# Relays, loads and the norm's product handed to other engines, in a talking-heads attention with an MLP

## The chip, the core and the metric

The kernel runs on one core of one Trainium2 chip. The time is the device time of one execution in microseconds. The profile that is read here is one execution as the hardware profiler recorded it; its engines are PE (TensorE matmul), PEld (TensorE weight load), DVE (VectorE), ACT (ScalarE), POOL (GpSimd) and SP (SyncE). A name like SPq or POOLq means the engine's instruction queue, where DMA issues and waits stand.

## What is computed

q, k and v have 4 batches, 12 heads, 448 positions and 64 columns. Before and after the softmax, the 12 heads are mixed by a 12 x 12 matrix; the result goes through an MLP of 768 to 2048 to 768 with a leaky ReLU whose slope is learned.

```python
scores = scale * np.matmul(q, k.transpose(0, 1, 3, 2))
scores = np.einsum('bhij,hg->bgij', scores, w_pre)
attn = np.exp(scores - np.max(scores, axis=-1, keepdims=True))
attn = attn / (np.sum(attn, axis=-1, keepdims=True) + 1e-09)
attn = np.einsum('bhij,hg->bgij', attn, w_post)
x = np.matmul(attn, v)            # then to (1792, 768)
h = x @ w_in
out = (np.maximum(h, 0.0) + alpha * np.minimum(h, 0.0)) @ w_out
```

## The kernel before, in words

The query rows of a batch are cut into chunks: seven of 60 rows and one of 30 (it starts at row 418 and overlaps the one before). 32 chunks follow one another. The kernel is written as a loop over steps n; the order of the instructions on every engine is the order in which the loop writes them, and the framework adds the semaphore waits.

**Scores.** `qk(ci, p)` (L178) makes a third of a chunk's raw scores by matmuls (L185) and copies them from PSUM to `s_t[ci]` ("st") on ACT (L189). st has two buffers, so the copy for chunk ci waits until all relays have read chunk ci-2. In st a partition holds one query row of one half of the heads.

**Relays.** Mixing heads is a matmul whose contraction runs over heads, so heads and a few query rows must lie on partitions. `relay(n, dmas)` (L193) does this with DMAs from SBUF to SBUF: for group n (10 query rows, 12 heads) two transfers u = 0, 1 of 60 rows of 1792 bytes each take rows of st into `sr_b` ("sr"), six buffers in turn. For the short chunk, whose second half lies 60 partitions on, each transfer is made as two of 30 rows (L206, otherwise L203). At step n `relays(2*(n+RA+1), ...)` issues the two groups that the mix three steps later will read (RA = 3). There are 180 groups, two per step. All transfers of the loop stand on SP; the first four groups are shared by SP and ACT.

**Mix, exp, norm, post.** `mix(n)` (L210) multiplies two groups by `wk` (L213) and takes the negated row maximum on DVE (nm, L215). `exp(n)` (L217) runs on ACT and also gives the row sums. `norm(n-1)` (L568) adds 1e-9 and takes the reciprocal on DVE (L571, L572) and multiplies it into the second mixing matrix (r, L575): on GpSimd as long as the MLP's first tile is in work (`cur == 0`, which holds for 87 of 90 steps), on DVE after it. `post(n-2)` (L227) multiplies exp by r (L235) and copies the result to `a_t` on ACT (L241, L246).

**pv.** At the steps in `pv_at`, 16 times, `pv(due, hx)` multiplies by v (L258), adds two halves on ACT and DVE (xe, L271, L272), and leaves a store to the DRAM tile x2 (L275) in a list, `later`; `flush()` issues it on SP in the next step, behind the relays.

**Loads.** `load_q` (three buffers), `load_k` (one buffer for each p) and `load_v` (one for each hx) are issued on GpSimd. k and q for later chunks go through the list `loads`, which is worked off in the step after the qk that frees the buffer; the next batch's v is issued right behind the `pv` that frees it.

**Weights.** The MLP's weights come as 64-bit floats. `convert()` reads raw pieces by GpSimd DMAs (cr, L292), turns them into 32-bit floats by instructions on DVE (L60, L64 to L67) and GpSimd (L61, L62), and stores them to a DRAM tile wsc (L301). `load_w` reads them back (wr, L343) and `split_w` splits them into a rounded part (ACT, L356) and a rest (GpSimd, L357), "ws".

**MLP.** `moe(t)` is a generator for one batch (tile t): first matmul L413, second L447, three products of parts for each. `moe_work(n, amount)` runs it on until the step's budget of estimated PE time is used: PACE = 2000 ns a step while the first tile is in work, then 5400. It begins at a step after `ready[0]` (26 here), when the x of the first batch has been stored and read back (xr, L463) and split on DVE (xs, L476, L477). As long as `lead` holds, a step has no MLP work and four pieces of convert. What of the MLP is left after step 94 is run to its end alone.

A step writes, in this order: mix(n), relays, flush, loads, norm(n-1), pv if due, post(n-2), exp(n), qk, MLP and convert work. On GpSimd a step's queue therefore holds: loads of k and q, r, loads of v, then the weights' wr, ws, ce, wsc and cr.

Of the kernel before, what the change touches and what calls it, by code (L numbers as in the profile page):

```python
# [19 lines left out]
B, H, S, D = 4, 12, 448, 64  # L20
DM, DFF = 768, 2048
NT = B * S
HI = 5
# [4 lines left out]
CW = 60  # L28
# [42 lines left out]
def talking_heads_prelu(ctx: ExitStack, tc: tile.TileContext, q, k, v, w_pre, w_post, mask, w_in, w_out, alpha, out):  # L71
# [81 lines left out]
        age[next(i for i in range(4) if pairs[i] is t)] = clock[0]  # L153
        clock[0] += 1

    def load_k(b, p, dma=nc.gpsimd):
        k_t[b, p] = kp.tile([128, 2, S], F32, tag=f"k{p}", name=f"k{b}_{p}")
        src = k[b].rearrange("d (c r p j) -> r p d c j", r=2, c=2, j=S)
        for r in range(2):
            (dma if dma else (nc.sync, nc.scalar)[r]).dma_start(out=k_t[b, p][64 * r:64 * r + 64], in_=src[r, p])  # L160

    def load_q(ci, dma=nc.gpsimd):
        b, c = chunks[ci]
        n = NP * CHUNKS[c][1]
        q_t[ci] = q_b[ci % 3]
        src = q[b, :, q_off[c]:q_off[c] + 2 * n].rearrange("d (c r x) -> r d c x", c=2, r=2)
        for r in range(2):
            (dma if dma else (nc.sync, nc.scalar)[r]).dma_start(
                out=q_t[ci][64 * r:64 * r + 64, SR0:SR0 + n].rearrange("d (c x) -> d c x", c=2), in_=src[r])

    def load_v(b, hx):
        t = v_t[b, hx] = vp.tile([128, NS, DM // 2], F32, tag=f"v{hx}", name=f"v{b}_{hx}")
        nf = S // 128
        cols = slice(hx * (DM // 2), (hx + 1) * (DM // 2))
        nc.gpsimd.dma_start(out=t[:, :nf, :], in_=v[b, :nf * 128, cols].rearrange("(s p) n -> p s n", p=128))
        nc.gpsimd.dma_start(out=t[:S - nf * 128, nf, :], in_=v[b, nf * 128:, cols])

    def qk(ci, p, copy=nc.scalar.copy):  # L178
        b, c = chunks[ci]
        pt = grab()  # L180
        cn = CHUNKS[c][1]
        for cc in range(2):
            for r in range(2):
                h = slice(64 * r, 64 * r + 64)
                nc.tensor.matmul(pt[64 * cc:64 * cc + 64, r, :S], q_t[ci][h, (3 * cc + p) * cn + SR0 * cc:(3 * cc + p) * cn + SR0 * cc + 64],  # L185
                                 k_t[b, p][h, cc, :], start=True, stop=True)
        if p == 0:
            s_t[ci] = sp.tile([128, 2, 3, S], F32, tag="s", name=f"st{ci}")
        copy(s_t[ci][:, :, p, :], pt[:, :, :S])  # L189
        free(pt)  # L190
        done_qk.add((ci, p))
# [3 lines left out]
    def relay(n, dmas):  # L195
        ci, g = groups[n]
        nh = half(ci)
        t = sr_t[n] = sr_b[n % NSR]
        for u in range(2):
            p, o = SR0 + 2 * g + u, SR0 + HP * u  # L200
            dma = dmas[u % len(dmas)]
            if nh * HI == CW:
                dma.dma_start(out=t[o:o + HP], in_=s_t[ci][p:p + nh * (GI - 1) + 1:nh])  # L203
            else:
                for c in range(2):
                    dma.dma_start(out=t[o + HP // 2 * c:o + HP // 2 * (c + 1)], in_=s_t[ci][p + CW * c:p + CW * c + nh * (HI - 1) + 1:nh])  # L206

    def mix(n):
        to = m_t[n] = grab()
# [291 lines left out]
    with tc.manual_schedule():  # L501
# [37 lines left out]
            in1=wb[:, 1, :].rearrange("p (o g) -> p o g", o=1).to_broadcast([128, HI, H]),  # L539
            op=ALU.mult,  # L540
        )
        load_q(1)
        nc.gpsimd.dma_start(out=alpha_sb, in_=alpha)
        conv = convert()
        relayed = 0
# [22 lines left out]
        def norm(n):  # L568
            se = se_t.pop(n)
            s1 = sm.tile([128, 2], F32, tag="s1", name=f"s1{n}")  # L570
            nc.vector.tensor_scalar_add(s1, se, 1e-9)  # L571
            nc.vector.reciprocal(out=s1, in_=s1)  # L572
            r = rp.tile([128, 2, HP], F32, tag="r", name=f"r{n}")
            wf = wq.rearrange("p (o g) i -> p o (g i)", o=1)
            (nc.gpsimd if cur == 0 else nc.vector).tensor_tensor(r, wf.to_broadcast([128, 2, HP]),  # L575
                                    s1.rearrange("p (u o) -> p u o", o=1).to_broadcast([128, 2, HP]), ALU.mult)
            r_t[n] = r

        def moe_work(n, amount):
            nonlocal cur, budget  # L580
            budget += amount
            while budget > 0 and cur < len(TB):
                if tasks[cur] is None:
                    if n <= ready[cur] + 1:
                        budget = 0.0
                        return
                    for _ in (nxt_x[cur] if cur in nxt_x else split_x(cur)):
                        pass
                    if cur == 1:
                        converts(conv_steps)  # L590
                        cvs.close()
                        wops.append(ctx.enter_context(tc.tile_pool(name="wop2", bufs=2, reuse_waits="tile")))
                    tasks[cur] = moe(cur)
# [5 lines left out]
        def step(n):  # L599
            step_now[0] = n  # L600
            if n in (0, 1):
                load_q(n + 2)
            if n in (2, 3):
                load_v(0, n - 2)
            due = pv_at.get(n)
            lead = n <= ready[0] + 1
            pace = 0.0 if lead else PACE[min(cur, 2)]
            if live(n):
                mix(n)
            if n >= 0:  # L610
                relays(2 * (n + RA + 1), (nc.sync,))
            flush()
            for f, *args in loads:
                f(*args)
# [3 lines left out]
            if due is not None:  # L618
                b = pvs[due][0]
                for hx in range(2):  # L620
                    pv(due, hx)
                    if due + 1 < len(pvs) and pvs[due + 1][0] != b:
                        load_v(b + 1, hx)
            if live(n - LAG):
                post(n - LAG)
            if live(n):
# [74 lines left out]
```

## Time and profile before

| what | us |
|---|---|
| runs, median (lowest to highest of 3) | 1000.92 (992.66 to 1004.43) |
| the profiled execution | 996.11 |
| its span from first to last instruction | 994.3 |

The mean granted TensorE clock of the profiled execution was 0.945 of full speed. In the rows below, times are microseconds from the span's start unless marked ns. A row of a wait reads: engine and what it was about to do, then after the arrow what ended the wait, the sum in us, how often, and the longest. The names before and after an arrow of an instruction are what it writes and what it reads.

### The profile page before, as it was taken

What the parts mean: (1) busy time and instruction counts of PE and PEld (TensorE: products, weight loads), DVE (VectorE), ACT (ScalarE), POOL (GpSimd) and SP (SyncE); (2) the same over time, 40 slices, a digit from 0 to 9 for tenths busy, and PEclk for the clock granted to TensorE, in tenths of its full rate; (3) what the DMA queues carried; (4) which work ended last, traced back from release to release, by engine and by line L of the source; (5) the groups of instructions that cost most, each with busy time, mean ns of one, the idle gap of its engine ahead of it and who ended that gap; (6) DMA issues with size and microseconds to landing.
All of it is one profiled execution on the core that took longest, in us unless ns stands there. A gap on an engine that the chain in (4) does not pass through costs nothing.

```text
span 994.3 us, 27470 instructions
## 1 busy us (share of the span) xinstructions
PE 859.1 (86%) x11532; PEld 666.7 (67%) x11532; DVE 598.4 (60%) x990; ACT 429.1 (43%) x780; POOL 561.8 (57%) x713
## 2 busy tenths in 40 slices
PE   6688666587889979787799988999999999999997
PEld 2354444254647657464566657899988999889996
DVE  4468545468657788873665444645476565764564
ACT  2357455435456556453465753523223233133231
POOL 6456535626667675765572411556664766567661
PEclk7789889869989999897999999999999999999999
DMA  6777757736687686676665534343346433444422
GB/s 176 193 217 221 185 159 249 217 117 192 183 213 232 191 264 190 202 194 174 190 196 162 161 118 164 93 124 112 107 115 186 127 112 110 125 152 119 111 80 72
DMA packets 74603, 161.71 MB, mean 163 GB/s; under 512 B 26277, under 2 KB 56113, under 8 KB 74481
## 3 DMA queue, kind: packets, MB, share of 16 engines
q0 software_dynamic: 25408, 103.16, 37.2%
q1 hardware_dynamic: 48216, 55.59, 17.9%
q8 instruction: 91, 1.49, 0.6%
q10 hardware_dynamic: 856, 1.21, 0.4%
q14 instruction: 32, 0.25, 0.1%
HBM read 97.62 MB, written 23.59 MB: 122 GB/s over the span
## 4 chain that ended last, share of the span: by engine, by line
PE 54%; DMA 15%; DVE 14%; POOL 8%; issue 5%; ACT 3%; SPq 0%; POOLq 0%; ACTq 0%; DVEq 0%
PE p L413 19%; PE p L447 17%; DMA sr<-st 8%; PE p L258 7%; PE p L235 4%; PE p L213 4%; PE p L185 4%; POOL ws L357 3%; DVE nm L215 2%; DMA xr<-x 2%; DVE acc L379 2%; DMA x<-xe 1%; DVE g L371 1%; DVE xs L477 1%; DVE t L364 1%
## 5 line engine op out<-in xcount | busy, mean ns | idle before, releaser
L357 POOL TENSOR_TENSOR ws<-wr,ws 128x768 fp32r<-128x768 f32 x128 | 236.7, 1850 | 179.0 <-ACT ws L356 178.1
L413 PE MATMUL p<-xs,ws 128*128 128x448 f32 x1152 | 254.0, 374 | 9.8 <-DVE xs L476 9.4
L447 PE MATMUL p<-g,ws 128*128 128x448 f32 x1152 | 247.4, 370 | 8.6 <-POOL ws L357 5.2
L413 PEld LDWEIGHTS p<-xs,ws 128*128 128x128 f32 x1152 | 216.3, 191 | 53.1 <-issue 27.0
L447 PEld LDWEIGHTS p<-g,ws 128*128 128x128 f32 x1152 | 215.7, 189 | 39.2 <-POOL ws L357 7.9
L356 ACT CAST ws<-wr 128x768 fp32r<-128x768 f32 x128 | 104.0, 838 | 196.0 <-issue 114.1
L235 PEld LDWEIGHTS p<-r,e 64*64 64x64 f32 x5040 | 104.0, 138 | 80.8 <-POOL r L575 50.4
L215 DVE TENSOR_REDUCE nm<-p 128x2 f32<-128x896 f32 x90 | 97.7, 1085 | 90.1 <-PE p L213 87.4
L185 PE MATMUL p<-k,q 64*64 64x448 f32 x768 | 113.5, 610 | 37.6 <-ACT st L189 14.8
L235 PE MATMUL p<-r,e 64*64 64x60 f32 x5040 | 110.1, 226 | 37.6 <-POOL r L575 27.8
L222 ACT ACTIVATE e<-p,nm 128x448 f32<-128x448 f32 x180 | 112.6, 635 | 59.0 <-DVE nm L215 38.8
L241 ACT COPY at<-p 128x960 f32<-128x960 f32 x88 | 86.7, 985 | 106.1 <-PE p L235 104.9
L213 PE MATMUL p<-sr,wk 64*64 64x448 f32 (+1 forms) x720 | 109.1, 597 | 24.4 <-DMA sr<-st 12.2
L364 DVE TENSOR_SCALAR t<-p,alpha_sb 128x448 f32<-128x448 f32 x64 | 43.4, 679 | 139.2 <-PE p L413 139.2
L379 DVE TENSOR_TENSOR acc<-p,acc 128x896 f32<-128x896 f32 x84 | 90.4, 1084 | 41.7 <-PE p L447 41.7
L189 ACT COPY st<-p 128x896 f32<-128x896 f32 x95 | 84.5, 912 | 70.4 <-DMA sr<-st 55.6
L575 POOL TENSOR_TENSOR r<-wq,s 128x120 f32<-128x120 f32 x87 | 38.4, 442 | 130.2 <-DVE s L572 108.3
L258 PEld LDWEIGHTS p<-at,v 64*64 64x64 f32 x2688 | 82.3, 141 | 20.9 <-ACT e L222 9.4
L343 POOL DMA_DIRECT2D wr<-wsc x128 | 72.0, 563 | 42.5 <-POOL ws L357 30.8
L258 PE MATMUL p<-at,v 64*64 64x120 f32 (+1 forms) x2688 | 84.9, 273 | 10.4 <-ACT e L222 5.5
L371 DVE TENSOR_TENSOR g<-t,g 128x448 fp32r<-128x448 f32 x64 | 74.2, 1200 | 2.1 <-ACT g L370 2.1
L213 PEld LDWEIGHTS p<-sr,wk 64*64 64x64 f32 (+1 forms) x720 | 28.2, 141 | 66.4 <-issue 23.4
(49 smaller groups left out, 676.8 us busy)
## 6 DMA issues: line engine op xcount, KB each, us to landing
wr<-wsc POOLq DMA_DIRECT2D x128, 384.0 KB, 3.5
sr<-st SPq DMA_DIRECT2D x332, 105.0 KB
cr<-in_w_in_dram POOLq DMA_DIRECT2D x32, 384.0 KB, 6.0
cr<-in_w_out_dram POOLq DMA_DIRECT2D x32, 384.0 KB, 5.2
wsc<-ct POOLq DMA_DIRECT2D x64, 192.0 KB, 4.2
xr<-x SPq DMA_DIRECT2D x24, 224.0 KB
out_dram<-acc SPq DMA_DIRECT2D x12, 448.0 KB
q<-in_q_dram POOLq DMA_DIRECT2D x54, 90.0 KB, 5.2
```

Of the source, the lines that this page charges most:

```text
L185: nc.tensor.matmul(pt[64 * cc:64 * cc + 64, r, :S], q_t[ci][h, (3 * cc + p) * cn + SR0 * cc:(3 * cc + p) * cn + SR0 * cc + 64], k_t[b, p][ ...
L213: nc.tensor.matmul(to[hf:hf + 64, u, :S], wk[r, :], g[r, :], start=True, stop=True)
L215: nc.vector.tensor_reduce(out=nm, in_=to[:, :, :S], axis=AX.X, op=ALU.max, negate=True)
L222: nc.scalar.activation(out=e_t[n][:, u], in_=m_t[n][:, u, :S], func=AF.Exp, bias=nm_t[n][:, u:u + 1], scale=1.0, accum_out=se_t[n][:, u:u ...
L235: nc.tensor.matmul(dst[:, :, HI * u:HI * u + HI], e[h, u, 64 * jb:64 * jb + 64], r[h, u].rearrange("p (h i) -> p h i", h=H), start=True, s ...
L241: nc.scalar.copy(at[:, :, col:col + 2 * GI].rearrange("p q (g i) -> p g q i", g=2), pt[:, :, :NS * GP].rearrange("p g (q i) -> p g q i", i ...
L258: nc.tensor.matmul(to[64 * t:64 * t + 64, r, cl * cn:(cl + 1) * cn], v_t[b, hx][pr, s, (2 * cl + t) * D:(2 * cl + t + 1) * D], a_t[pr, s, ...
L356: nc.scalar.copy(t[:, 0], w)
L357: nc.gpsimd.tensor_tensor(t[:, 1], w, t[:, 0], ALU.subtract)
L379: nc.vector.tensor_tensor(dst, pt[:, :, :N], dst, ALU.add)
L413: nc.tensor.matmul(pt[:, f % 2, :S], w[:, tw, c * 128:(c + 1) * 128], xs[:, tx, c, :], start=(j == 0), stop=(j == 3 * NCC - 1))
L447: nc.tensor.matmul(pt[:, d, :S], w[:, tw, (c + d) * 128:(c + d + 1) * 128], g[:, tg], start=(j == 0), stop=(j == 3 * FG - 1))
```

## The change

Five things are changed. (1) In the loop, relays are issued with the list (SP, GpSimd): transfer u = 0 of each group on SP, u = 1 on GpSimd. (2) q of a short chunk is loaded 30 columns further on, so that its rows in st lie in one regular pattern, and the short chunk's transfer is one of 60 rows, not two of 30. (3) q, k and v are issued on SP, all through the list `loads`, which a step works off behind its relays and its x stores; the load of chunk 1's q before the loop stays on GpSimd. (4) norm's product is always on DVE. (5) The MLP's first work and the end of `lead` come one step later.

```diff
-    def load_k(b, p, dma=nc.gpsimd):
+    def load_k(b, p, dma=nc.sync):
...
-    def load_q(ci, dma=nc.gpsimd):
+    def load_q(ci, dma=nc.sync):
...
-                out=q_t[ci][64 * r:64 * r + 64, SR0:SR0 + n].rearrange("d (c x) -> d c x", c=2), in_=src[r])
+                out=q_t[ci][64 * r:64 * r + 64, 64 - CHUNKS[c][1]:64 - CHUNKS[c][1] + n].rearrange("d (c x) -> d c x", c=2), in_=src[r])
...
-        nc.gpsimd.dma_start(out=t[:, :nf, :], in_=v[b, :nf * 128, cols].rearrange("(s p) n -> p s n", p=128))
-        nc.gpsimd.dma_start(out=t[:S - nf * 128, nf, :], in_=v[b, nf * 128:, cols])
+        nc.sync.dma_start(out=t[:, :nf, :], in_=v[b, :nf * 128, cols].rearrange("(s p) n -> p s n", p=128))
+        nc.sync.dma_start(out=t[:S - nf * 128, nf, :], in_=v[b, nf * 128:, cols])
...
         for u in range(2):
-            p, o = SR0 + 2 * g + u, SR0 + HP * u
-            dma = dmas[u % len(dmas)]
-            if nh * HI == CW:
-                dma.dma_start(out=t[o:o + HP], in_=s_t[ci][p:p + nh * (GI - 1) + 1:nh])
-            else:
-                for c in range(2):
-                    dma.dma_start(out=t[o + HP // 2 * c:o + HP // 2 * (c + 1)], in_=s_t[ci][p + CW * c:p + CW * c + nh * (HI - 1) + 1:nh])
+            p, o = 64 - CHUNKS[chunks[ci][1]][1] + 2 * g + u, SR0 + HP * u
+            dmas[u % len(dmas)].dma_start(out=t[o:o + HP], in_=s_t[ci][p:p + nh * (GI - 1) + 1:nh])
...
-        load_q(1)
+        load_q(1, nc.gpsimd)
...
-            (nc.gpsimd if cur == 0 else nc.vector).tensor_tensor(r, wf.to_broadcast([128, 2, HP]),
+            nc.vector.tensor_tensor(r, wf.to_broadcast([128, 2, HP]),
...
-                    if n <= ready[cur] + 1:
+                    if n <= ready[cur] + 2:
...
             if n in (0, 1):
-                load_q(n + 2)
+                loads.append((load_q, n + 2))
             if n in (2, 3):
-                load_v(0, n - 2)
+                loads.append((load_v, 0, n - 2))
...
-            lead = n <= ready[0] + 1
+            lead = n <= ready[0] + 2
...
-                relays(2 * (n + RA + 1), (nc.sync,))
+                relays(2 * (n + RA + 1), (nc.sync, nc.gpsimd))
...
-                        load_v(b + 1, hx)
+                        loads.append((load_v, b + 1, hx))
```

## Rows read from the trace of the kernel before

**Rows 1.** The page: busy time of each engine, and granted clock in 40 slices

```profile
PE 859.1 (86%) x11532; PEld 666.7 (67%) x11532; DVE 598.4 (60%) x990; ACT 429.1 (43%) x780; POOL 561.8 (57%) x713
...
PEclk7789889869989999897999999999999999999999
```

**Rows 2.** Busy time by stretch: length; PE, PEld, DVE, ACT, POOL; clock, DMA share, GB/s

```profile
30.00:180.00 150.00, 107.73 (x2496) 69.95 (x2496) 86.46 (x184) 82.38 (x164) 82.32 (x140) 0.86 0.70 203
180.00:215.00 35.00, 19.60 (x275) 12.53 (x273) 15.57 (x34) 9.09 (x19) 12.22 (x22) 0.66 0.67 198
215.00:600.00 385.00, 327.71 (x6086) 227.37 (x6081) 255.28 (x463) 211.14 (x406) 223.84 (x329) 0.96 0.65 188
...
650.00:994.00 344.00, 335.33 (x1777) 307.46 (x1769) 197.33 (x228) 94.90 (x134) 210.01 (x172) 1.00 0.41 118
```

**Rows 3.** The chain that ended last: shares by engine, then pieces (start, us, what)

```profile
PE 54%; DMA 15%; DVE 14%; POOL 8%; issue 5%; ACT 3%; SPq 0%; POOLq 0%; ACTq 0%; DVEq 0%
...
117.42 14.09 DMA sr<-st
...
444.07 14.54 DMA sr<-st
```

**Rows 4.** Who waited for whom, the whole span: us in total, times, longest

```profile
POOL r L575 <- DVE s L572: 108.3, 37, 16.4
...
ACT st L189 <- DMA sr<-st: 55.6, 10, 13.8
...
PE p L235 <- POOL r L575: 27.8, 17, 4.5
...
PE p L185 <- ACT st L189: 14.8, 4, 7.5
...
PE p L213 <- DMA sr<-st: 12.2, 4, 4.8
...
PE p L185 <- DMA k<-in_k_dram: 10.9, 6, 4.2
...
PE p L213 <- ACT st L189: 4.3, 3, 2.3
```

**Rows 5.** Groups of instructions, shapes apart: busy us, mean ns | idle before

```profile
L215 DVE TENSOR_REDUCE nm<-p 128x2 f32<-128x896 f32 x90 | 97.7, 1085 | 90.1 <-PE p L213 87.4 <-ACT ws L356 2.6
...
L575 POOL TENSOR_TENSOR r<-wq,s 128x120 f32<-128x120 f32 x87 | 38.4, 442 | 130.2 <-DVE s L572 108.3 <-PE p L185 14.7 <-PE p L258 5.8
...
L168 POOL DMA_DIRECT2D q<-in_q_dram x62 | 38.2, 626 | 15.9 <-PE p L185 8.1 <-DMA v<-in_v_dram 2.3 <-PE p L258 2.0
...
L175 POOL DMA_DIRECT2D v<-in_v_dram x8 | 6.2, 776 | 0.0
L176 POOL DMA_DIRECT2D v<-in_v_dram x8 | 4.4, 552 | 0.0
...
L575 DVE TENSOR_TENSOR r<-wq,s 128x120 f32<-128x120 f32 x3 | 0.8, 283 | 0.2
```

**Rows 6.** Tile sr, its instructions: ns min/median/max, first and last start

```profile
L213 PEld LDWEIGHTS p<-sr,wk x720: 129/133/228, 18.1 to 628.4; 64*64 64x64 f32 x169, 60*64 60x64 f32 x11
...
L203 SPq DMA_DIRECT2D sr<-st x332: 762/767/1647, 12.4 to 613.7; - x166
L206 SPq DMA_DIRECT2D sr<-st x48: 741/746/773, 122.1 to 479.1; - x48
```

**Rows 7.** DMA issues on the page: count, KB each, us from issue to landing

```profile
q<-in_q_dram POOLq DMA_DIRECT2D x54, 90.0 KB, 5.2
```

**Rows 8.** DMA queues from 108 to 132 us: packets, MB, share of 16 engines

```profile
q0 software_dynamic: 1008, 3.74, 59.4%
q1 hardware_dynamic: 1726, 1.78, 26.9%
...
k<-in_k_dram POOLq DMA_DIRECT2D x6, 224.0 KB, 9.5
...
q<-in_q_dram POOLq DMA_DIRECT2D x2, 90.0 KB, 9.3
```

More of the change, by code (lines that the diff above doesn't have):

```diff
@@ L184, in qk @@
                 h = slice(64 * r, 64 * r + 64)
-                nc.tensor.matmul(pt[64 * cc:64 * cc + 64, r, :S], q_t[ci][h, (3 * cc + p) * cn + SR0 * cc:(3 * cc + p) * cn + SR0 * cc + 64],
+                nc.tensor.matmul(pt[64 * cc:64 * cc + 64, r, :S], q_t[ci][h, (3 * cc + p) * cn + (64 - cn) * cc:(3 * cc + p) * cn + (64 - cn) * cc + 64],
                                  k_t[b, p][h, cc, :], start=True, stop=True)
```

## The prediction, made before the change was run

> **What bounds the kernel now.** I read the page first, then the busy time of each engine by stretch, the chain of waits, the list of who waited for whom, the groups of instructions, and last the DMA queues.
>
> The page shows PE busy for 859.1 of 994.3 us, and DVE and POOL near 60% [rows 1]. The mean hides two different stages. From 650 us on only the MLP is left: PE is busy for 335 of 344 us at full clock [rows 2], and nothing that the diff touches runs there. Before that the attention runs, with some MLP work put between its steps by a fixed budget. From 30 to 180 us PE is busy for 107.7 of 150 us, from 180 to 215 us for 19.6 of 35, from 215 to 600 us for 327.7 of 385: idle 42, 15 and 57 us. DMA is 65 to 70% busy in all three, and PE's granted clock is below full in the first two (0.86 and 0.66) [rows 1, 2]. So whatever the change gains lies in these 115 us of idle PE and in the lower clock beside them. PE's work itself is only moved in time: what isn't done between steps is done after them.
>
> The chain shows where the idle time comes from. DMA holds 15% of it, and its longest pieces are waits for relays of some 14 us, as at 117 and 444 us [rows 3]. The waits give the totals. ACT's copies into st (L189) waited 55.6 us for relays to have read the old st. PE idled 27.8 us for r from POOL (17 times), 14.8 and 4.3 us for those st copies, 12.2 us for sr directly and 10.9 us for k [rows 4]: 70 us that the change aims at by its place. All sums below are made against the profiled execution's own 996.11 us, which is 0.5% under the median of the runs, 1000.92.
>
> **Part 1: norm's product from POOL to DVE.** It removes 87 instructions from POOL, 38.4 us, and adds 87 to DVE at the 283 ns that three such instructions already take there: 24.6 us [rows 5]. The product's inputs come from DVE itself, so a hop between engines goes too, and r no longer stands behind POOL's subtractions (ws) and DMA issues. What reads r is post(n-2), one step later; on DVE r is ready a step before it. Of the 27.8 us of PE idle I count 20 as gained, since in the lead-in, where the chain runs through DVE itself, the next wait is close behind. Bounds: 0 to -28. The price is DVE time. DVE has 14% of the chain, 139 of its 598 busy us [rows 1, 3], so 23% of an added microsecond lies on the path: 24.6 x 0.23 = +6 us. Bounds: 0 (all hidden beside PE) to +24.6 (all of it on the path).
>
> **Part 2: half of the relays begun by POOL, short chunks in one transfer.** There are 384 relay transfers now: 332 and 48 on SP, 4 on ACT [rows 6]. The 48 halves become 24, so 360. The first six groups keep 12 on SP and ACT; of the other 348, SP and POOL begin 174 each. On SP a step's four relays take 4 x 0.767 = 3.07 us to issue one after the other, and for the short chunks eight halves take 8 x 0.746 = 5.97 us [rows 6]; with two on each of two engines it is 1.53 us on SP. What is released last, the st copy or the sr that mix reads, comes some 1.5 us earlier, and 4.4 us earlier in a short chunk's steps.
>
> On POOL the trace has no relay. Its DMA issues take 552 to 776 ns by the rows of v, and 626 for q [rows 5]; I take 0.60 us, near q's, the transfer nearest in size: 174 x 0.60 = 104 us (96 to 135). Taken off POOL: 38.4 us of products and the issues of 60 q, 18 k and 16 v, 94 x 0.626 = 58.8 us by q's row. Net +7 us of 562 busy (-1 to +38), so POOL is hardly fuller. It gets no longer wait either: now it waits 108.3 us in all, 37 times, for DVE's reciprocal before r [rows 4], which on DVE stands behind the reduction of the same step's mix. A relay on POOL waits for the mix alone, which is earlier. Behind it queue POOL's ws subtractions and wr loads, the same that queue behind r now.
>
> What lies on the path: 14.8 + 4.3 + 12.2 = 31.3 us of PE idle from relays. The long stalls are where transfers on POOL's queue crowd the relays' queue. From 108 to 132 us POOL's queue q0 holds the 16 DMA engines 59.4% of the time and SP's q1 26.9% [rows 8], and six k loads and two q loads were issued on q0 there. Afterwards k, q and v stand on q1, half of the relays on q0, and every step's relays ahead of that step's loads. I count half of the 31.3, -16 us; bounds 0 to -31 if the transfers only change places, and above zero as the second rival has it.
>
> The Trainium skill speaks against this part. "DMA: Bandwidth & Descriptors" (Rules for kernel authors) says that spreading DMAs over SP, ACT and GpSimd doesn't help bandwidth, as all run on the same 16 engines, and saves only issue time. The trace agrees that both queues share the engines (59.4% and 26.9% in one window); it doesn't show yet whether order alone removes a 14 us stall. By the rule the -16 would be only the issue time, and this is the first rival.
>
> **Part 3: q, k and v on SP behind the step's relays and stores.** 94 issues leave POOL and stand on SP: 94 x 0.77 = 72 us on an engine that keeps 182 of its 380 relay issues (174 and 8 ahead of the loop) and so loses 198, 152 us. POOL's own waits before such loads go too: 8.1 us before q, and 14.7 us that L575 waited for L185's matmuls, which k and q loads ahead of it wait for [rows 5]. On SP a load waits for matmuls of the previous step; the next step's relays, queued behind it, need the later mix anyway. k must still land before the next chunk's scores: of its 10.9 us I count -3 (bounds +10.9, as much again if k waits behind relays and stores on one queue, to -10.9).
>
> **Part 4: one more step of lead.** The MLP starts one step later, so 2000 ns (PACE[0]) of PE work move behind the attention: +2 us and no more. Less if that work met a PE that idled anyway: the other bound is -15, all idle PE of 180 to 215 us, where the MLP starts [rows 2].
>
> **Clock.** The 107.7 us of PE work from 30 to 180 us ran at a granted 0.86, so for part of the time at 1.2 GHz and not 2.4; at full clock it would be some 15 us shorter, and the lower level stands in the stretches with most idle PE [rows 2]. I take -4 (0 to -15). **New lateness.** Relays on POOL's queue stand behind wr and cr loads there. A 90 KB q load on it landed 5.2 us after issue [rows 7], and POOL is at times a step late. I take +5, a quarter of the 19.1 us that PE idled for the st copies (0 to the second rival's size).
>
> Sum: -20 + 6 - 16 - 3 + 2 - 4 + 5 = -30 us, so 966 us against the profile, a ratio of 0.970. On the median of 1000.92 that is **970 us**, the prediction. The terms' own spread makes this case 955 to 985.
>
> **Rivals.**
> 1. *Bytes bound the relays.* For it: the DMA engines were 86% busy in the window above [rows 8], and no byte is taken away. Against: over the attention the share is 65 to 70% [rows 2], and the stalls are few and long. Then the relay and k terms vanish (+19), and so does the clock's (+4) and the new lateness (-5): -12 us, 989 on the median.
> 2. *POOL's relays come too late; slower.* Place: the st copy of each chunk, L189, mostly one step after the last relays of the chunk two before. A step is about 6.8 us (90 mixes from 18.1 to 628.4 us [rows 6]), and that copy comes into the next one, behind a reduction of 1.1 us [rows 5] and two exps (I put 3 us for it all), so it decides from where a POOL relay lands over 9 us after its mix. For it: r stands where these relays will stand in POOL's order, and PE met it late 17 times [rows 4]; 5.2 us of landing leaves little [rows 7]. Against: POOL waited for DVE at that point 37 times, so it was in time then. If each of 30 chunks waits 5 us there, ACT's wait goes from 55.6 to 150 us. PE idled 19.1 of those 55.6 us, a third, so PE's idle grows by 32: -20 + 6 + 2 + 32 = +20, 1021. "SBUF — State Buffer" (the engine ports) of the Trainium skill names a mechanism that would add to this: GpSimd can't write a DMA's descriptors while VectorE holds a port that they share. The rows so far don't show it in the issue times, 552 to 776 ns on average with DVE 60% busy [rows 1, 5].
> 3. *More than counted.* The 70 us of aimed waits go nearly whole, with the clock: -28 + 6 - 31 - 8 + 2 - 8 = -67 by the bounds; -55 taken as reachable, 946.
> 4. *Nothing.* The r wait is replaced by one for DVE's longer queue and relays stay as they are: -10 + 6 + 2, 999.
>
> **How the numbers follow.** Forecast 0.47, rival 1 0.18, rival 2 0.17, rival 3 0.12, rival 4 0.06. Over 1% either way (991 and 1011) is about what a measurement of this kernel can tell from no change, as its three runs lie 1.2% apart. The forecast and rival 3 are faster; of rival 1, which sits at the edge, 0.12, in all 0.71. Same: 0.06 of rival 1, 0.05 of rival 2 in a mild form and 0.05 of rival 4, in all 0.16. Slower: the rest of rival 2 and a little of rival 4, 0.13. The range leaves out half of rival 3 and two thirds of rival 2, together under 2 in 10: 945 to 1004.
>
> **What would show it.** Right: L575 on DVE 90 times at about 283 ns and PE's wait for r under 5 us; POOL with 174 relay issues near 0.6 us and about as busy as now; ACT's wait for relays at L189 under 30 us, with no piece of over 10 us in the chain; granted clock before 215 us higher; the MLP from its lone stage on unchanged in length. Wrong: a landing of POOL's relays over 9 us, L189 waiting over 55 us, or idle PE before DVE's max reduction (nm) grown by the added DVE work; unchanged long relay pieces with DMA share unchanged mean rival 1.

## The result and the profile after

The changed kernel takes 1010.84 us (median of 13 runs, 1003.47 to 1019.48), against 997.92 for the kernel before in the runs beside it. The ratio is 1.0132, 95% interval 1.0097 to 1.0168: slower by 1.3%, on the other side of no change than the forecast of 970 and outside its range. The profiled execution took 1003.47 us, its span 1001.7. It is the shortest of the 13, so the two profiles lie 7.4 us apart where the medians lie 12.9 apart.

A ratio on record takes only the runs within 1.5% of a kernel's shortest, and beside e5 to e12 one very short run of the kernel before (984.6 and 984.8 us) therefore makes the cut drop 16 of its 29 and 7 of its 17 runs, which puts these eight ratios 0.4 to 0.6% too high beside the others. So a second figure stands with a ratio where it matters: "by all runs" is the mean of all runs of a kernel over that of the kernel before beside it, which lies between 997.4 and 1000.0 us each time. For the changed kernel it is 1.0139; outside e5 to e12 the two figures differ by 0.12% at most.

The page of the kernel after (busy time; granted clock; shares of the chain that ended last; the issues of relays on POOL) answers to [rows 1, 3, 7].

```profile
PE 866.3 (86%) x11532; PEld 673.7 (67%) x11532; DVE 619.8 (62%) x1077; ACT 429.4 (43%) x780; POOL 565.0 (56%) x706
...
PEclk7689899689889999898988998999999999999999
...
PE 47%; DMA 15%; DVE 13%; issue 11%; POOL 9%; ACT 3%; SPq 1%; POOLq 0%; ACTq 0%; DVEq 0%
...
sr<-st POOLq DMA_DIRECT2D x174, 105.0 KB, 5.7
```

Span less busy time gives PE's idle time: 135.4 us after, 135.2 before. It has not shrunk, and the same 11532 matmuls kept PE busy 7.2 us longer, at a mean granted clock of 0.934 where it was 0.945. DMA still holds 15% of the chain.

By stretch (columns as in [rows 2]), the kernel after:

```profile
30.00:180.00 150.00, 113.95 (x2664) 72.49 (x2656) 96.50 (x224) 88.15 (x178) 87.53 (x147) 0.90 0.79 215
180.00:215.00 35.00, 18.02 (x333) 13.82 (x333) 18.44 (x44) 10.55 (x23) 10.36 (x18) 0.66 0.63 180
215.00:600.00 385.00, 329.64 (x5936) 229.21 (x5935) 266.50 (x502) 204.85 (x392) 221.15 (x320) 0.93 0.67 183
...
650.00:994.00 344.00, 340.36 (x1808) 311.85 (x1807) 202.91 (x233) 96.02 (x136) 215.29 (x177) 1.00 0.41 118
```

Ahead of 180 us the change works: 2664 matmuls instead of 2496 in the same 150 us, at a higher clock. From 215 to 600 us 150 fewer are done (5936 for 6086), at a lower clock, and what is missing is done at the end. So a gain and a loss lie in different stages. Not all of either is the relays' doing; the experiments part them.

Who waited for whom, the kernel after (us in total, times, longest), answering to [rows 4]:

```profile
POOL ws L352 <- ACT ws L351: 214.0, 77, 20.8
...
POOL sr L201 <- PE p L208: 44.9, 18, 7.0
...
ACT st L189 <- DMA sr<-st: 37.3, 8, 8.8
...
PE p L208 <- DMA sr<-st: 18.8, 8, 4.6
...
PE p L185 <- ACT st L189: 16.3, 4, 6.2
...
PE p L230 <- ACT st L189: 11.8, 3, 4.7
...
PE p L185 <- DMA k<-in_k_dram: 11.1, 6, 5.4
PE p L253 <- ACT st L189: 9.2, 3, 4.5
PE p L230 <- DVE r L570: 8.9, 8, 3.9
```

PE's wait for r fell from 27.8 to 8.9 us. In its place PE waits for the st copies: L230 (post) and L253 (pv) together 21.0 us, where before only pv had such a wait, one of 2.5 us; and L185 16.3. The relays themselves cost PE 18.8 us for 12.2. And POOL's longest wait is for ACT's casts, before its ws subtraction: 214.0 us. POOL waited for a mix before a relay only 18 times in 87 steps (44.9 us); mostly the mix had ended before POOL came to its relays. In the view that gave [rows 4], the wait for the casts was already POOL's largest, a row that the prediction did not read; the second row is pv's one wait:

```profile
POOL ws L357 <- ACT ws L356: 178.1, 74, 12.2
...
PE p L258 <- ACT st L189: 2.5, 1, 2.5
```

The st copies and r by form, and the relays of tile sr, kernel after, answering to [rows 5, 6]; the first row is the kernel before, whose row for the st copies [rows 5] leaves out:

```profile
L189 ACT COPY st<-p 128x896 f32<-128x896 f32 x95 | 84.5, 912 | 70.4 <-DMA sr<-st 55.6 <-PE p L185 4.5 <-DMA x<-xe 4.0
...
L189 ACT COPY st<-p 128x896 f32<-128x896 f32 x95 | 84.7, 913 | 91.2 <-DMA sr<-st 37.3 <-DMA k<-in_k_dram 18.6 <-PE p L185 12.7
...
L570 DVE TENSOR_TENSOR r<-wq,s 128x120 f32<-128x120 f32 x90 | 28.2, 313 | 3.1
```

```profile
L201 SPq DMA_DIRECT2D sr<-st x182: 762/790/1781, 13.9 to 616.5; - x182
L201 POOL DMA_DIRECT2D sr<-st x174: 547/586/782, 35.7 to 614.2; - x174
...
DMA to landing us min/median/max: 2.1/5.7/10.1
```

ACT's idle time before L189 grew from 70.4 us to 91.2, though the part that relays end by the profile fell from 55.6 to 37.3. POOL's issues cost what was forecast, 0.589 us each; their landing reaches 10.1 us (the trace has the landings of POOL's transfers, not of SP's).

What that looks like in one stretch of the timeline of the kernel after (start, length, engine; an issue "x2" is two transfers):

```profile
518.43 0.98 PE L208 MATMUL p<-sr,wk 64*64 64x448 f32 x8
...
519.42 1.62 SPq L201 DMA_DIRECT2D sr<-st  x2
...
519.58 1.82 POOL L352 TENSOR_TENSOR ws<-wr,ws 128x768 fp32r<-128x768 f32 x1 [10.20 <-ACT ws L351]
...
522.30 1.85 POOL L352 TENSOR_TENSOR ws<-wr,ws 128x768 fp32r<-128x768 f32 x1
...
523.04 0.98 PE L208 MATMUL p<-sr,wk 64*64 64x448 f32 x8
...
523.48 0.53 SPq L175 DMA_DIRECT2D v<-in_v_dram  x1
...
525.08 1.19 POOL L201 DMA_DIRECT2D sr<-st  x2
...
526.11 0.54 SPq L176 DMA_DIRECT2D v<-in_v_dram  x1
...
526.76 1.76 SPq L201 DMA_DIRECT2D sr<-st  x2
...
529.77 1.18 POOL L201 DMA_DIRECT2D sr<-st  x2
...
533.14 1.71 ACT L189 COPY st<-p 128x896 f32<-128x896 f32 x2 [5.95 <-DMA sr<-st]
...
534.10 1.86 PE L230 MATMUL p<-r,e 64*64 64x60 f32 x54 [4.17 <-ACT st L189]
```

The mix of a step ends at 519.41. SP begins its two relays 0.01 us later. POOL's two stand in its queue behind two ws subtractions, the first of which has waited 10.20 us for ACT's casts, and are begun at 525.08, 5.67 us later. The next mix ends at 524.02. Now SP is late too, since it is issuing loads of v until 526.65: its relays begin at 526.76, POOL's at 529.77. At 533.14 the st copy has waited 5.95 us for a relay to finish, and post's matmuls start at 534.10 after PE has idled 4.17 us for that copy.

Counted over steps 27 to 86 of the timeline, from the end of a step's mix to the end of its last relay's issue, median and 90th percentile: in the kernel after 1.7 and 4.1 us on SP, 5.3 and 11.9 us on POOL; with all four relays on SP (e6, below) 3.8 and 8.8. In steps 0 to 26, ahead of the MLP, the medians after are 2.2 on SP and 4.0 on POOL, and 6.6 in e6. So POOL is late in both stages. Ahead of the MLP four relays on SP alone are later still; after its start they are not.

What stands in front of POOL's relays can be counted too. Over steps 27 to 86 of the kernel after, the time from the end of a mix to the start of POOL's first relay is 291 us in all, 4.1 at the median. Of it 84 us go to the conversion's ce (29 of them waiting for DVE), 78 to ws (21 waiting for ACT's casts), 99 to issues of wr, wsc and cr, and 23 to relays of the step before. So the MLP's own ws and wr are 117 us of it, and the conversion (ce, wsc, cr), which stands in the queue ahead of the MLP too, is half.

### The profile page after: what moved, and what is told of

It reads as the page before. It is cut to its first block, busy times and chain, and to the rows that moved or that the text cites. A ratio compares the mean times of both kernels' runs of the same rounds, so it can differ in the third digit from the quotient of the medians.

```text
span 1001.7 us, 27286 instructions
## 1 busy us (share of the span) xinstructions
PE 866.3 (86%) x11532; PEld 673.7 (67%) x11532; DVE 619.8 (62%) x1077; ACT 429.4 (43%) x780; POOL 565.0 (56%) x706
## 4 chain that ended last, share of the span: by engine, by line
PE 47%; DMA 15%; DVE 13%; issue 11%; POOL 9%; ACT 3%; SPq 1%; POOLq 0%; ACTq 0%; DVEq 0%
PE p L408 17%; PE p L442 16%; DMA sr<-st 5%; PE p L253 4%; POOL ws L352 4%; PE p L230 3%; PE p L185 3%; DMA xr<-x 3%; PE p L208 3%; DMA cr<-in_w_out_dram 3%; DVE nm L210 2%; DMA k<-in_k_dram 2%; POOL sr L201 1%; DVE acc L374 1%; DMA wr<-wsc 1%
## 5 line engine op out<-in xcount | busy, mean ns | idle before, releaser
L352 POOL TENSOR_TENSOR ws<-wr,ws 128x768 fp32r<-128x768 f32 x128 | 236.3, 1846 | 215.0 <-ACT ws L351 214.0
L408 PE MATMUL p<-xs,ws 128*128 128x448 f32 x1152 | 251.3, 372 | 1.8 <-DVE xs L471 0.8
L230 PEld LDWEIGHTS p<-r,e 64*64 64x64 f32 x5040 | 107.8, 140 | 65.0 <-issue 28.6
L185 PE MATMUL p<-k,q 64*64 64x448 f32 x768 | 118.0, 631 | 37.7 <-ACT st L189 16.3
L201 POOL DMA_DIRECT2D sr<-st x174 | 100.6, 589 | 73.5 <-PE p L208 44.9
L230 PE MATMUL p<-r,e 64*64 64x60 f32 x5040 | 112.6, 228 | 25.8 <-ACT st L189 11.8
L208 PE MATMUL p<-sr,wk 64*64 64x448 f32 (+1 forms) x720 | 109.4, 593 | 24.8 <-DMA sr<-st 18.8
L189 ACT COPY st<-p 128x896 f32<-128x896 f32 x95 | 84.7, 913 | 91.2 <-DMA sr<-st 37.3
L253 PE MATMUL p<-at,v 64*64 64x120 f32 (+1 forms) x2688 | 88.7, 279 | 29.0 <-ACT e L217 16.0
L253 PEld LDWEIGHTS p<-at,v 64*64 64x64 f32 x2688 | 85.1, 145 | 39.5 <-ACT e L217 18.8
L61 POOL TENSOR_SCALAR ce<-ce 128x384 int32<-128x384 int32 x64 | 35.4, 554 | 80.7 <-DVE ce L60 78.0
```

The costliest lines, as they stand in the source:

```text
L201: dmas[u % len(dmas)].dma_start(out=t[o:o + HP], in_=s_t[ci][p:p + nh * (GI - 1) + 1:nh])
L208: nc.tensor.matmul(to[hf:hf + 64, u, :S], wk[r, :], g[r, :], start=True, stop=True)
L230: nc.tensor.matmul(dst[:, :, HI * u:HI * u + HI], e[h, u, 64 * jb:64 * jb + 64], r[h, u].rearrange("p (h i) -> p h i", h=H), start=True, s ...
L253: nc.tensor.matmul(to[64 * t:64 * t + 64, r, cl * cn:(cl + 1) * cn], v_t[b, hx][pr, s, (2 * cl + t) * D:(2 * cl + t + 1) * D], a_t[pr, s, ...
L352: nc.gpsimd.tensor_tensor(t[:, 1], w, t[:, 0], ALU.subtract)
L408: nc.tensor.matmul(pt[:, f % 2, :S], w[:, tw, c * 128:(c + 1) * 128], xs[:, tx, c, :], start=(j == 0), stop=(j == 3 * NCC - 1))
```

## The experiments

All ratios are to the kernel before on the same chip, with 95% intervals. A quotient of two of them carries about 0.005 to 0.006 either way.

**Each part alone, then all but one.** Edits are the parts of the diff above. For r on DVE alone (e1), and for the relays (e2) alone:

```
-            (nc.gpsimd if cur == 0 else nc.vector).tensor_tensor(r, ...
+            nc.vector.tensor_tensor(r, ...
...
-                relays(2 * (n + RA + 1), (nc.sync,))
+                relays(2 * (n + RA + 1), (nc.sync, nc.gpsimd))
```

> The kernel before, with only norm's product moved to DVE for all steps. Theory A (relays begun by GpSimd land too late; the product's move is a gain): 8 to 20 us faster than before, PE's wait for r below 10 us. Theory B (loads on SP hold up the relays behind them; the product's move is about neutral): within 5 us. Theory C (DVE's queue is what got longer): 5 to 10 us slower, ACT's wait for nm in exp grown from 39 us to over 50.

> The kernel before, with only the second transfer of each group begun by GpSimd in the loop (short chunks still in halves). Theory A: 15 to 30 us slower than before, GpSimd's relays landing in 5 us or more at the median and ACT's wait for relays at L189 at or above 56 us. Theory B: within 5 us of before, as the relays alone are not what was held up. Theory C: within 5 us.

> The kernel before, with only q, k and v loaded by SP behind each step's relays and stores. Theory A: within 5 us, or faster by up to 10 as GpSimd loses 94 issues and its waits for L185. Theory B: 10 to 20 us slower, with relays queued behind k and v in the chain. Theory C: within 5 us.

> The kernel before, with only the first MLP work and the end of lead one step later. Theories A and B: 0 to 3 us slower (2000 ns of PE work moved behind the attention). Theory C, in which the pacing is what costs: 5 to 10 us slower.

> The kernel before, with only the short chunk's q moved and its relays made in one transfer of 60 rows. Theory A2 (the single parts are harmless or helpful except the relays on GpSimd, and the loss of the whole change is their interplay): 0 to 6 us faster, as 24 issues of 0.75 us go. Theory D (the short chunk's new shape itself is slow, for it puts all of a transfer's rows on another pattern): 5 to 15 us slower.

Measured: r alone 0.9857 [0.9815, 0.990]; half of the relays on POOL alone 1.0088 [1.005, 1.0127]; q, k, v on SP alone 0.9978 [0.995, 1.0007]; one more step of lead alone 1.0023 [0.9987, 1.0058]; short chunks in one transfer alone 1.0053 [1.0011, 1.0095], which by all runs is 0.9996 (± 0.003), so a cost of these transfers is not shown. Added up they make no change on record (-1.4 + 0.9 - 0.2 + 0.2 + 0.5 = 0.0%) and -0.4% by all runs, and all together cost 1.3%.

r does what was forecast. The waits of e1:

```profile
PE p L185 <- DMA k<-in_k_dram: 9.5, 6, 4.5
...
PE p L235 <- DVE r L575: 5.7, 6, 1.7
```

and of e2, where r still stands on POOL:

```profile
PE p L235 <- POOL r L575: 63.6, 27, 5.8
...
ACT st L189 <- DMA sr<-st: 15.7, 3, 8.9
```

There the relays do shorten ACT's wait, 55.6 to 15.7 us, but r, behind relay issues on POOL, makes PE wait 63.6 us for 27.8. Theory A had e1 right and the direction of e2, but had expected 15 to 30 us lost there (9 measured) and ACT's wait at 56 us or more. Theory B's loss of 10 to 20 us from the loads alone is not there.

> The changed kernel with the loop's relays all on SP again. Theory A2: 10 to 20 us faster than the kernel before, close to norm's product alone (987). Theory E (r on DVE loses its gain as soon as loads stand on SP): within 5 us of the kernel before or slower.

> The changed kernel with q, k and v loaded by GpSimd again at their old places, relays still half on GpSimd. Theory A2: slower than the kernel before by 0 to 10 us, so the loss stands with the relays. Theory F (loads on SP and half of the relays on GpSimd are each harmless and collide only together): 10 to 15 us faster than the kernel before, since e2 lost its time in r on GpSimd, which is on DVE here.

> The changed kernel with norm's product on GpSimd again while the first tile is in work. Theory A2: 15 to 30 us slower than the kernel before, PE's wait for r over 50 us. Theory G (r on DVE is worth nothing once the relays stand on GpSimd): the same time as the changed kernel within 5 us.

Measured: the change without relays on POOL (all on SP) 0.9945 [0.990, 0.9991], by all runs 0.990; without the loads on SP 0.9981 [0.9934, 1.0028], by all runs 0.993; without r on DVE 1.0266 [1.0201, 1.033], by all runs 1.021. Beside the other parts, relays on POOL cost 1.9% on record (1.0132 / 0.9945) and 2.4% by all runs; the loads on SP cost 1.5% and 2.1%; r gains 1.3% and 0.7% (each by all runs ± 0.5 or 0.6). e6 lies between theories A2 and E on record and near A2 by all runs (10 us faster); e7 fits neither A2 nor F; e8 is as slow as A2 said, with a wait of PE for r of 48.9 us.

**Which property of the relays: k loads in their way, their number, or the engine?** Theory F1 held that the k loads now on SP delay relays, F2 that each relay on POOL costs. Edits to the changed kernel: k back on POOL (e9); the relays' second queue on ACT (e10); all relays on POOL (e11).

```
+    def load_k(b, p, dma=nc.gpsimd):
...
+                relays(2 * (n + RA + 1), (nc.sync, nc.scalar))
...
+                relays(2 * (n + RA + 1), (nc.gpsimd,))
```

> The changed kernel with k alone loaded by GpSimd again; q and v stay on SP. Theory F1 (the loss is that SP's relays stand behind bulk loads of k on SP's queue while GpSimd's queue, now with relays beside the weights, takes more of the DMA engines): half or more of the 1.3% comes back, within 5 us of the kernel before. Theory F2 (a relay begun by GpSimd lands late whatever SP carries, and that is all): no change against the changed kernel, 8 to 18 us slower than before.

> The changed kernel with the second transfer of each group begun by ACT instead of GpSimd. F1 and F2 both expect GpSimd's queue to be as free as in the run without relays on it; ACT pays 174 issues of 0.8 us, 139 us on an engine 43% busy. If two queues for relays are worth anything by themselves, 5 to 15 us faster than before; if ACT's issue time and its waits for the mix stand in the way of exp and the copies, 10 us slower or more.

> The changed kernel with both transfers of each group begun by GpSimd in the loop, SP left with loads and stores: the dose doubled. F2: about twice the loss that the GpSimd relays cost with loads on SP (1.9%), so 25 us slower than before or more, ACT's idle before L189 over 110 us. F1: no relay stands behind k any more, so no slower than the changed kernel, within 5 us of it.

Measured: e9 1.0172 [1.0119, 1.0224], e11 1.0165 [1.0115, 1.0216], e10 1.0136 [1.0066, 1.0205]; by all runs 1.011, 1.011 and 1.009, against 1.014 for the change. e9 gives back 0.3% by all runs (± 0.5), not half of the loss, so F1 falls. In e11 twice the relays on POOL cost no more that can be measured, so F2 falls; that a step which waits for one late relay is not made later by a second would explain it and was not tested. e10 takes about the same time with a new wait. Its issues take ACT 0.79 us each, and PE now waits for ACT's copies of at:

```profile
PE p L230 <- ACT at L236: 18.0, 8, 6.5
PE p L185 <- ACT at L236: 15.2, 7, 5.0
```

**The loads, with r out of the way.** e12 is the kernel before with r on DVE and q, k, v on SP.

> The kernel before with norm's product on DVE and q, k and v on SP; relays all on SP, short chunks in halves, lead as before: the two parts that weren't slower alone. If they add: 12 to 20 us faster than before (0.980 to 0.988). If the loads take away what the product gives: within 5 us.

Measured 0.9956 [0.9926, 0.9986], by all runs 0.991. So once r is on DVE the loads cost 1.0% on record (e12 / e1), but 0.4 ± 0.5% by all runs, which is not clear of the error. PE's wait for k is longer than the 9.5 us of e1, in e12 and then in e6:

```profile
PE p L185 <- DMA k<-in_k_dram: 14.1, 3, 9.6
```

```profile
PE p L185 <- DMA k<-in_k_dram: 21.7, 8, 7.7
```

It does not explain the loss: it is 11.1 us in the kernel after, where the loads cost most, and 15.9 in e7, where POOL loads k. With r on POOL the loads did help r a little: PE's wait for it is 21.7 us in e3, 27.8 before.

**Where the relays lose.** Theory P: a relay on POOL is late only where the MLP's ws and wr stand in POOL's queue. Theory Q: the loss is an interplay of the parts, in both stages. e13 and e14 split the changed kernel at the start of the MLP; e15 is the change without relays on POOL and without the loads.

```
+                relays(2 * (n + RA + 1), (nc.sync, nc.gpsimd) if lead else (nc.sync,))
...
+                relays(2 * (n + RA + 1), (nc.sync,) if lead else (nc.sync, nc.gpsimd))
```

> The changed kernel with half of the relays begun by GpSimd only as long as lead holds (steps 0 to 28), all on SP after it. Theory P (GpSimd reaches its relays late only when the MLP's subtractions and weight loads stand in the same queue: its issue ended 4.0 us after the mix at the median before step 27 and 5.3 us after it, SP's 1.7 us): the loss is gone and the lead-in's gain of some 8 us stays, 10 to 20 us faster than the kernel before. Theory Q (bulk loads on SP run beside the other queue's relays, in all steps alike): the loss goes down by the share of the steps, two thirds, to about the time of the kernel before.

> The changed kernel with half of the relays begun by GpSimd only from step 29 on, all on SP before. Theory P: as slow as the changed kernel or slower by up to 8 us, 13 to 21 us slower than before. Theory Q: one third of the loss goes, 5 to 9 us slower than before.

> The kernel before with norm's product on DVE, the short chunk in one transfer and the later start of the MLP: what the changed kernel is without both its new queues. If the parts add, 0.993 of before (0.986 + 0.005 + 0.002), 7 us faster; then relays on GpSimd cost 0.5% without the loads on SP and 1.9% with them, and the loads 0.1% and 1.5%. At 0.986 or less, short and lead cost nothing beside the product, and relays on GpSimd cost 1.2% without the loads already; at 1.000 or more, they eat what the product gives and the interplay of the two queues shrinks to under 1%.

Measured: POOL's relays ahead of the MLP alone 0.9892 [0.9848, 0.9935]; after its start alone 1.0127 [1.008, 1.0173], the whole loss of the change. Against none (e6) the first is a gain of 0.5% on record and 0.2 ± 0.6% by all runs, not clear of the error. The two were measured beside each other, differ by 2.4% (e14 / e13, ± 0.5), and only in the stage: the loss stands behind the MLP's start, as theory P forecast and Q did not. P's reason holds in part only, by the counts above: POOL's relays are late ahead of the MLP too (4.0 us), and ws and wr are not the most of what stands in front. POOL's landings do not make the difference between the stages: their median is 6.4 us in e13, where these relays cost nothing, and 4.9 in e14. The relays on tile sr and the page's busy row, in e13:

```profile
PE 855.4 (87%) x11532; PEld 666.4 (68%) x11532; DVE 617.8 (63%) x1077; ACT 428.8 (44%) x780; POOL 497.3 (51%) x590
```

```profile
L201 POOL DMA_DIRECT2D sr<-st x58: 549/589/724, 36.8 to 184.3; - x58
```

and in e14, with its waits of PE for the st copy:

```profile
PE 875.3 (86%) x11532; PEld 677.2 (67%) x11532; DVE 624.8 (62%) x1077; ACT 429.0 (42%) x780; POOL 530.5 (52%) x648
```

```profile
PE p L230 <- ACT st L189: 11.5, 3, 5.1
...
PE p L253 <- ACT st L189: 8.8, 2, 4.6
```

The spans are 979.0 and 1014.2 us, so PE idled 123.6 us in e13 and 138.9 in e14: 15.3 us. The other 19.9 us of the difference is PE busy longer with the same matmuls, at a clock of 0.928 for 0.944. This pair overstates it: e14's profile is its longest run and e13's its shortest, 35.1 us apart where the medians lie 23.1 apart, and the clock over the six runs of each is 0.932 for 0.940. That the idle time lowers the clock was not tested. Post and pv wait 20.3 us for the st copy in e14, 21.0 in the kernel after, 2.0 (pv alone) in e13.

e15 came to 0.9844 [0.9805, 0.9884], by all runs 0.983. So without the loads the relays cost 1.4% on record and 0.9% by all runs (e7 / e15), and the loads without the relays 1.0% and 0.7% (e6 / e15), each by all runs ± 0.5. The sum is 2.4% or 1.6%; the change's distance from e15 is 2.9% (1.0132 / 0.9844 = 1.029) or 3.1%. What is missing, 0.5% on record, is within the error, but by all runs 1.4 ± 0.7% comes only with both together. The traces of these four kernels, one execution each, speak for the second (us; mixes are counted from 0):

| kernel | relays on | loads on | end of mix 27 | from there to the end of mix 89 |
|---|---|---|---|---|
| e15 | SP | POOL | 174.4 | 437.3 |
| e7 | SP and POOL | POOL | 165.7 | 451.9 |
| e6 | SP | SP | 174.0 | 434.2 |
| after | SP and POOL | SP | 170.7 | 460.2 |

With the loads on POOL, relays on POOL gain 8.7 us ahead of the MLP and lose 14.6 after; with the loads on SP they gain 3.3 and lose 26.0. So the loads on SP take from the gain and add to the loss. How they do so was not found: the last relay of a step is issued no later in the kernel after than in e7 (5.3 and 5.6 us at the median), and SP's share as soon (1.7 and 1.6), so that a stretch like the one above, with SP held up by v, is the exception.

**Which relays, and through which wait?** L189 needs the last relays of a chunk. e17 keeps a chunk's last two groups on SP, e18 puts only these on POOL.

```
+            (nc.sync if g >= nh // 2 - 2 else dmas[u % len(dmas)]).dma_start(...
...
+            (nc.sync if g < nh // 2 - 2 else dmas[u % len(dmas)]).dma_start(...
```

> The changed kernel, but the last two groups of each chunk, whose reading frees st, are relayed by SP alone; two thirds of GpSimd's relays stay. If the loss is the st copies (L189) waiting for GpSimd's late relays of a chunk's end: ACT's idle time before L189 falls from 91 us to 75 or less, and the time to within 0.5% of the kernel before (over half of the 1.9% comes back). If it is GpSimd's own time or relays that land late at the mix: two thirds of it stays, 1.006 of before or slower.

> The opposite: GpSimd begins the second transfer of the last two groups of each chunk alone, one third of its relays. If the st copies are the place: ACT's idle time before L189 stays near 90 us and half or more of the loss stays with a third of the relays, 1.004 to 1.013 of before. If not: a third of the 1.9% stays, about 1.000.

Measured: e17 1.0028 [0.9993, 1.0063] with 112 relays on POOL, e18 1.0014 [0.9982, 1.0046] with 62. Against none (e6) they cost 0.8% and 0.7% on record, 1.3% and 1.0% by all runs (± 0.5), against the change's 1.9% and 2.4%. e17 meets what was expected of the st copies in both numbers; e18 stays under its 1.004, with 81.4 us of idle before L189. In e17 that idle time is the lowest of the runs that put relays on POOL in the changed kernel, and post waits for no st copy:

```profile
L189 ACT COPY st<-p 128x896 f32<-128x896 f32 x95 | 84.9, 915 | 59.9 <-DMA sr<-st 26.8 <-DMA q<-in_q_dram 19.3 <-PE p L185 11.0
```

while e18, with about half as many relays there, has these waits back:

```profile
PE p L230 <- ACT st L189: 10.4, 3, 4.7
...
PE p L253 <- ACT st L189: 4.8, 2, 4.3
```

So the st copy is likely one of the places where late relays are paid. It is not the only one: e17 still loses 0.8% (1.3% by all runs) without it, and where that goes stays open. Nor does its wait set the time alone: in e11 ACT's idle before L189 is 97.7 us and the kernel no slower. A third buffer for st, which would test L189 by itself, was not tried.

**A better version.** e16 is the kernel before with r on DVE and half of the relays on POOL in the lead alone (e13's line).

> A version put together from the runs: the kernel before with norm's product on DVE and half of the relays begun by GpSimd only while lead holds; loads, short chunks and the MLP's start as before. Theory P: 0.975 to 0.983 of the kernel before (the product's 1.4% and part of the 8 us of the lead-in), the fastest so far. Theory Q: 0.986 to 0.992.

Measured 0.9789 [0.9747, 0.983], 977.12 us: 2.1% under the kernel before, and the best of all. Of that about 0.7% is the relays (e16 / e1, ± 0.6), just clear of the error. Its page and its stretches from 30 and from 215 us:

```profile
PE 854.7 (88%) x11532; PEld 663.8 (68%) x11532; DVE 619.2 (64%) x1077; ACT 427.9 (44%) x780; POOL 555.5 (57%) x688
```

```profile
30.00:180.00 150.00, 109.45 (x2632) 71.18 (x2632) 93.03 (x216) 86.05 (x175) 110.23 (x187) 0.89 0.79 222
215.00:600.00 385.00, 331.62 (x6186) 231.18 (x6184) 271.34 (x516) 210.41 (x407) 192.06 (x266) 0.96 0.65 192
```

It has the kernel after's gain ahead of 180 us (2632 matmuls) without its loss behind 215 us (6186 for 5936), at the clock of 0.96 that the kernel before had there.

## Why the prediction was wrong

- **Part 1, r: right.** -20 + 6 = -14 us were forecast; e1 measured -1.43%, 14.3 us (13 by all runs). PE's wait for r fell by 22 us there, to 5.7 (20 forecast); it is 8.9 in the kernel after. r takes DVE 313 ns (283 forecast). What this costs DVE's path, forecast as +6, was not measured apart.
- **Part 2, the relays: the step that failed.** It said "A relay on POOL waits for the mix alone, which is earlier. Behind it queue POOL's ws subtractions and wr loads". Behind this step's relays they do, and so they stand in front of the next step's, with the conversion's ce and its issues. POOL works its queue off in order, as the timeline shows, and after the MLP's start its first relay begins 4.1 us (median) after its mix has ended, behind ws, ce and issues that are in work or waiting. "New lateness" named wr and cr loads alone and took +5 us; the relay term of -16 and this +5, -11 us together, were measured beside the other parts at +1.9% (after / e6), some 19 us, or 24 by all runs. The loss stands after the MLP's start. Ahead of it the traces show a gain of 3 to 9 us by mix 27, of which the times show 0.2 to 0.7%.
- **The reason given against it failed with it.** That POOL waited 37 times for DVE before r showed that POOL was in time for r, which comes behind the next reduction. A relay is due when the mix ends, earlier in the step, so being in time for r said nothing of it: POOL came before the mix's end only 18 times.
- **Rival 2 had the direction and the reason, not the size.** POOL's relays come too late: landings up to 10.1 us, and 5.3 us of median delay in POOL's queue before them. But ACT's wait for relays at L189 did not grow from 55.6 to 150 us; it fell to 37.3. PE's waits for the st copies rose from 21.6 us (14.8 + 4.3 + 2.5) to 39.4 (16.3 + 11.8 + 9.2, and 2.1 at L208), by about half of the 32 counted. Its 1021 lies above the measured 1011 also because it counted on a cost at every chunk and gave the lead no gain, and it left the loads at nothing. It had 0.17.
- **Part 3, the loads: wrong in sign, and the second step that failed.** -3 us were forecast. Beside relays on POOL they cost 1.5% on record (after / e7) and 2.1% by all runs, 15 to 21 us; without these relays 0.4 to 1.0% (e6 / e15, e12 / e1). "The next step's relays, queued behind it, need the later mix anyway" fails in the timeline above, where the mix ended at 524.02 and SP was still issuing v until 526.65, but such steps are few. PE's wait for k rose in e6 (21.7 us), not in the kernel after (11.1 for 10.9). What the loads' cost comes through stays open.
- **Short chunks:** 4.4 us earlier per step were counted within the relays' term; alone they measured +0.5% on record and 0.0% by all runs, and e15 stands where e1 does. **Lead:** +2 us, measured +0.2%, within the interval of no change.
- **Clock:** forecast -4. It rose ahead of 180 us (0.86 to 0.90) and fell from 215 to 600 us (0.96 to 0.93); PE was busy 7.2 us longer in all.
- **Rival 1** gave no sum that fits (989). Over the whole run neither ACT (e10) nor POOL with any share of the relays (e11, e17, e18) was faster than SP alone (e6); the wait moved to what the new engine had in its queue. The Trainium skill's "DMA: Bandwidth & Descriptors" (Rules for kernel authors) holds that another issuing engine saves issue time only. These runs agree that it brings no more, and they show that it can cost.

## What to carry to other kernels

Before a latency-critical transfer is moved to an engine that also computes, read what that engine waits for in front of it, the previous step's work included, and not only what the transfer itself waits for or what queues behind it. Bulk loads put on the queue of small urgent transfers cost 1.5 to 2.1% here beside the moved relays and nothing alone (e3), so a part that is harmless alone has to be tried with the others. Where stages differ, decide stage by stage: the same edit was 2.4% dearer after the MLP's start than ahead of it, and only the split showed it.

## What had not been expected of the hardware

The Trainium skill's "SBUF — State Buffer" (SBUF: two separate sides) lets some VectorE instructions lock GpSimd out of the port by which it writes a DMA's descriptors. Here the issue times show no such stall: 547 / 586 / 782 ns (least, median, most) over 174 relay issues with DVE 62% busy. The delay that was found lies in POOL's order; whether the landings are longer for that port no run shows. And the idle time was not the whole difference: between the traces of e13 and e14, 15.3 us of idle came with 19.9 us of slower matmuls, and over all their runs the clock is 0.940 and 0.932.
